# Batch 1's x loaded ahead of the weights, and its transposes and scores moved forward, in a cross-attention and maxout kernel

## The chip, the cores and the metric

The kernel runs on one core of a Trainium2 chip. Its time is the device time of one execution in microseconds; it stands as the median of several runs. The engines are named as the profile names them: PE (TensorE) for matmuls and transposes, with PEld for its weight loads, DVE (VectorE), ACT (ScalarE), POOL (GpSimd) and SP (SyncE, which here only issues DMAs).

## The reference

Attention in both directions between `x` (8 batches, 8 heads, 512 rows, 64 columns) and `state` (8, 8, 32, 64), and then a feed-forward layer with a maximum over three products:

```python
scores = scale * x @ state^T                    # per batch and head: 512 x 32
a      = softmax(scores, over the 32)
xread  = a @ state                              # 512 x 64
a2     = softmax(scale * state @ x^T, over the 512)
sread  = a2 @ x                                 # 32 x 64
attn   = concat([xread, sread], axis=rows)      # 544 rows, heads side by side: 512 columns
h      = max(attn @ w1, attn @ w2, attn @ w3)   # 512 -> 768
out    = h @ w_out                              # 768 -> 512
```

## The kernel before

Work goes by batch. For batch `b` the steps are these; the lines are those of the profile.

- `load_x(b)` (L70) loads x with a cast to bf16 through POOL's DMA queue. The x of batch 0 comes in two halves, one through SP as f32 (L79) that DVE casts (L392), one through POOL (L84).
- `x_transpose(b, g, copy)` (L159) transposes half of x on PE, eight 128x128 blocks into one PSUM tile; `copy`, on ACT or DVE, brings it to `xT` (L162). From batch 3 on `x_transpose_dma` does it by a DMA from SP's queue (L166).
- `scores(b, g0, g1)` (L180) multiplies xT with a block-diagonal form of the state (`bd`), and ACT takes the exponential into `e` (L185). `softmax` sums on DVE (`den`, L192), takes the reciprocal (`rden`, L194) and multiplies on POOL or DVE (`a`, L195).
- `a_transpose` (L206, copies L207) brings `a` to `aT`.
- `g_cols(b, ms)` (L281) multiplies the state with columns of the three weight matrices: G = state @ W. A column `m` stands for 128 of the 768, in all three matrices, and has one copy, of 128x768 (L287). Thereby xread @ W becomes aT @ G. `g_cols_fast` (L312, copies L317) is the same for the first column of batch 0, split between ACT and DVE. With `defer` a copy stands not at once but behind the first cast of the next maxout.
- `x_maxout(b, m)` (L327) makes the three products of one column, six matmuls into three PSUM tiles; ACT casts the first (L331), and two maxima on DVE follow (L334, L335), which give `ht`.
- `sread(b)` (L225) is the attention in the other direction; its result goes through a DMA transpose on SP's queue (L233). Its normaliser comes from a column of ones that stands behind x (L110).
- `ffn_out(b, j)` (L365) multiplies `ht` with `wout`, copies on ACT and stores.

The weights W1, W2, W3 come in four chunks of columns, three parts each (`load_w`, L104): chunks 0 and 1 have one column each, chunks 2 and 3 two. `keep_busy(n)` (L121) runs n matmuls of zeros.

Every engine works through its instructions in the order in which the program issues them. That order is written out by hand for batches 0 and 1; from batch 2 on a loop over `b` and six slots lays the next batch's preparation between the six maxouts of this one. PSUM tiles rotate in two rings: four tiles for tag `pw` (transposes, half scores, maxouts, sread, ffn) and two tiles for tag `two` (G columns, full scores, idle matmuls). A new tile waits until the last reader of the one four, or two, before it has ended.

The order by hand around the change, before:

```python
load_w(0); load_w(1); load_x(1)                     # POOL's queue, behind x of batch 0
...
softmax(0, 1, 2, nc.vector.tensor_mul); keep_busy(9)
a_transpose(0, 0, act); a_transpose(0, 1, dve)
g_cols_fast(0, 0); g_cols(0, (1,))
...
x_maxout(0, 0)
x_transpose(1, 0, act); x_transpose(1, 1, dve)
x_maxout(0, 1)
scores(1, 0, 1); scores(1, 1, 2)
```

Of the kernel before, what the change touches and what calls it, by code (L numbers as in the profile page):

```python
# [15 lines left out]
def kernel(  # L16
# [14 lines left out]
    nc = tc.nc  # L31
# [22 lines left out]
    dve, act, pool = nc.vector.tensor_copy, nc.scalar.copy, nc.gpsimd.tensor_copy  # L54
# [14 lines left out]
    def load_x(b):  # L69
        nc.gpsimd.dma_start(  # L70
            out=x_sb[b][:, 0:XW].rearrange("p (h jd) -> p h jd", h=H),
            in_=x[b].rearrange("h (p j) d -> p h (j d)", j=J))

    def x0_heads(g):
        return x[0].rearrange("(s g) (p j) d -> g p s (j d)", g=2, j=J)[g]
# [6 lines left out]
    ident = const.tile([128, 128], BF16, name="ident")  # L82
    make_identity(nc, ident)
    nc.gpsimd.dma_start(out=x0_sb[1], in_=x0_heads(1))  # L84

    chunks = ((0, 1), (1, 2), (2, 4), (4, 6))
    w_sb = wpool.tile([128, HS, NM * 384], BF16, name="w")
# [2 lines left out]
    def w_slices(t, c):  # L90
        m0, m1 = chunks[c]
        return t[:, :, 384 * m0:384 * m1].rearrange("p a (i mf) -> p a i mf", i=3)
# [7 lines left out]
    def load_w(c, parts=(0, 1, 2)):  # L100
        m0, m1 = chunks[c]
        for i in parts:
            w = (moe_w1, moe_w2, moe_w3)[i].rearrange("(kk p) f -> p kk f", p=128)
            nc.gpsimd.dma_start(out=w_slices(w_sb, c)[:, :, i, :], in_=w[:, :, m0 * 128:m1 * 128])  # L104

    load_w(0)
    load_w(1)
    load_x(1)
    for b in range(2):
        nc.gpsimd.memset(x_sb[b][:, XW:XW + D], 1.0)  # L110
    bds = [data.tile([128, 2, H, 2, Ns], BF16, name=f"bd{k}") for k in range(B // 2)]
    nc.vector.memset(bds[0], 0.0)

# [4 lines left out]
    def keep_busy(n):  # L118
        p = pp.tile([128, 1024], F32, tag="two", name="idle")
        for _ in range(n):  # L120
            nc.tensor.matmul(p[:, 0:512], zero[:, 0:128], zero, start=True, stop=True)  # L121


    def bd(b, h):
        return bds[b // 2][:, b % 2, h]
# [23 lines left out]
    def new(d, b, shape, name, bufs=2):  # L149
        d[b] = work.tile(shape, BF16, tag=name, bufs=bufs, name=name)  # L150

    def x_transpose(b, g, copy):

        if g == 0:
            new(xT, b, [128, H, 2, 128], "xT", bufs=3)
        p = pp.tile([128, HS, 2, 128], BF16, tag="pw", bufs=4, name="pxt")
        for s in range(HS):
            for jj in range(2):
                nc.tensor.transpose(  # L159
                    p[:, s, jj, :],  # L160
                    xv[b][:, 2 * s + g, 2 * jj:2 * jj + 2, :].rearrange("p j d -> p (j d)"), ident)
        copy(out=xT[b].rearrange("p (s g) j t -> p g s j t", g=2)[:, g], in_=p)  # L162
# [5 lines left out]
    def scores(b, g0, g1):  # L168
        n = g1 - g0
        if g0 == 0:  # L170
            new(e, b, [128, J, 2, HS, Ns], "e")
        if n == 2:
            p = pp.tile([128, J, n, HS, Ns], F32, tag="two", name="ps")
        else:
            p = pp.tile([128, J, n, HS, Ns], F32, tag="pw", bufs=4, name="psh")
        for jj in range(2):
            for g in range(g0, g1):
                for s in range(HS):
                    h = 2 * s + g
                    nc.tensor.matmul(  # L180
                        p[:, 2 * jj:2 * jj + 2, g - g0, s, :], xT[b][:, h, jj, :],
                        bd(b, h).rearrange("p c n -> p (c n)"),
                        start=(g == g0 and s == 0 and (n == 2 or jj == 0)),
                        stop=(g == g1 - 1 and s == HS - 1), skip_group_check=True)
        nc.scalar.activation(out=e[b][:, :, g0:g1], in_=p, func=AF.Exp, scale=scale)  # L185

    def softmax(b, g0, g1, mul):
        n = g1 - g0
        if g0 == 0:
            new(a, b, [128, J, 2, HS, Ns], "a")  # L190
        den = work.tile([128, J, n, HS], F32, tag=f"den{n}", name="den")
        nc.vector.reduce_sum(out=den, in_=e[b][:, :, g0:g1], axis=AX.X)  # L192
        rden = work.tile([128, J, n, HS], F32, tag=f"rden{n}", name="rden")
        nc.vector.reciprocal(out=rden, in_=den)  # L194
        mul(  # L195
            out=a[b][:, :, g0:g1].rearrange("p j g s n -> p j (g s) n"),
            in0=e[b][:, :, g0:g1].rearrange("p j g s n -> p j (g s) n"),
            in1=rden.rearrange("p j g s -> p j (g s)").unsqueeze(3).to_broadcast((128, J, n * HS, Ns)))

    def a_transpose(b, g, copy):  # L200

        if g == 0:
            new(aT, b, [128, J, 2, 128], "aT", bufs=3)
        p = pp.tile([128, J, 128], BF16, tag="pw", bufs=4, name="pat")
        for j in range(J):
            nc.tensor.transpose(p[:, j, :], a[b][:, j, g].rearrange("p s n -> p (s n)"), ident)  # L206
        copy(out=aT[b][:, :, g, :], in_=p)  # L207
# [31 lines left out]
    def flush_copies():  # L239
        while copies_due:  # L240
            copies_due.pop(0)()
# [30 lines left out]
    def g_cols(b, ms, copies=(act, act), defer=(False, False)):  # L272
        flush_copies()
        for m, copy, wait in zip(ms, copies, defer):
            if m == 0:
                new(G, b, [128, 2, NM * 384], "G", bufs=3)
            p = pp.tile([128, 2, 512], F32, tag="two", name="pg")
            pv = p[:, :, 0:384].rearrange("p g (i f) -> p g i f", i=3)
            for s in range(HS):
                for g in range(2):  # L280
                    nc.tensor.matmul(  # L281
                        pv[32 * s:32 * s + 32, g], bd(b, 2 * s + g)[64 * g:64 * g + 64, g, :],
                        m_cols(w_sb, m)[64 * g:64 * g + 64, s],
                        start=True, stop=True, tile_position=(64 * g, 32 * s))

            def place(m=m, pv=pv, copy=copy):
                copy(out=m_cols(G[b], m), in_=pv)  # L287

            if wait:
                copies_due.append(place)  # L290
            else:
                place()
# [12 lines left out]
    def g_cols_fast(b, m):  # L305

        if m == 0:
            new(G, b, [128, 2, NM * 384], "G", bufs=3)
        p = [pp.tile([128, 512], F32, tag="pw", bufs=4, name=f"pgf{g}") for g in range(2)]
        for s in range(HS):  # L310
            for g in range(2):
                nc.tensor.matmul(  # L312
                    p[g][32 * s:32 * s + 32, 0:384].rearrange("p (i f) -> p i f", i=3),
                    bd(b, 2 * s + g)[64 * g:64 * g + 64, g, :], m_cols(w_sb, m)[64 * g:64 * g + 64, s],
                    start=True, stop=True, tile_position=(64 * g, 32 * s))
        for g, copy in ((0, act), (1, dve)):
            copy(out=m_cols(G[b], m)[:, g], in_=p[g][:, 0:384].rearrange("p (i f) -> p i f", i=3))  # L317
# [19 lines left out]
    def x_maxout(b, m):  # L337
        maxout(b, m, 512,
               lambda i, k: m_cols(G[b], m)[:, k, i],
               lambda k: aT[b][:, :, k, :], 2)  # L340
# [52 lines left out]
    x_transpose(0, 0, dve)  # L393
    x_transpose(0, 1, dve)
    scores(0, 0, 1)
    load_w(2, (0, 1))
    softmax(0, 0, 1, nc.gpsimd.tensor_mul)
    scores(0, 1, 2)
    softmax(0, 1, 2, nc.vector.tensor_mul)
    keep_busy(9)  # L400
    a_transpose(0, 0, act)
    a_transpose(0, 1, dve)
    g_cols_fast(0, 0)
    g_cols(0, (1,))
    load_w(2, (2,))
    load_w(3)
    load_st(1, nc.gpsimd)
    load_x(2)
    x_maxout(0, 0)
    x_transpose(1, 0, act)  # L410
    x_transpose(1, 1, dve)
    x_maxout(0, 1)
    scores(1, 0, 1)
    scores(1, 1, 2)
    softmax(1, 0, 1, nc.gpsimd.tensor_mul)
    softmax(1, 1, 2, nc.gpsimd.tensor_mul)
    nc.gpsimd.dma_start(out=wout_sb, in_=moe_w_out.rearrange("(kk p) f -> p kk f", p=128))
    for k in range(2, B // 2):
        load_st(k, nc.gpsimd)
# [1 line left out]
    load_x(4)  # L421
    for b in range(2, B):
        nc.gpsimd.memset(x_sb[b][:, XW:XW + D], 1.0)
    sread(0)
    g_cols(0, (2, 3))
    g_cols(1, (0,))
    x_maxout(0, 2)
    a_transpose(1, 0, act)
    a_transpose(1, 1, act)
    g_cols(1, (1,))  # L430
    x_maxout(0, 3)
    x_maxout(1, 0)
    g_cols(0, (4, 5), defer=(False, True))
    x_maxout(1, 1)
    states_cast(1, pool)
    x_maxout(0, 4)
    sread(1)
    g_cols(1, (2, 3), defer=(False, True))
    x_maxout(0, 5)
    states(1, act)  # L440
    x_transpose(2, 0, dve)
    x_transpose(2, 1, act)
    x_maxout(1, 2)
    g_cols(1, (4, 5), defer=(False, True))
    x_maxout(1, 3)
    scores(2, 0, 2)
# [83 lines left out]
```

## Time and profile before

| | us |
|---|---|
| median of 5 runs | 159.21 |
| lowest to highest of them | 157.75 to 159.85 |
| the profiled execution, its own time | 158.32 |
| its span, first to last instruction | 156.5 |
| PE busy in the span | 147.1 |
| DVE, ACT, POOL busy | 98.1, 94.1, 50.5 |

How to read the views. A stage table gives, for a stretch of the span, each engine's busy time and its number of instructions, the granted clock of TensorE, the DMA share and the rate. A row of the timeline has start and duration in us, engine, line, operation, what is written and read, shapes and a count of merged instructions; in brackets the engine's idle time before it and what ended that. The duration of merged matmuls includes the modelled tail of the last one, so matmuls start sooner after each other than the durations say. In the chain of waits a row has start, length and the work on the path; a DMA stands there from issue to landing.

### The profile page before, as it was taken

What the parts mean: (1) busy time and instruction counts of PE and PEld (TensorE: products, weight loads), DVE (VectorE), ACT (ScalarE), POOL (GpSimd) and SP (SyncE); (2) the same over time, 40 slices, a digit from 0 to 9 for tenths busy, and PEclk for the clock granted to TensorE, in tenths of its full rate; (3) what the DMA queues carried; (4) which work ended last, traced back from release to release, by engine and by line L of the source; (5) the groups of instructions that cost most, each with busy time, mean ns of one, the idle gap of its engine ahead of it and who ended that gap; (6) DMA issues with size and microseconds to landing.
All of it is one profiled execution on the core that took longest, in us unless ns stands there. A gap on an engine that the chain in (4) does not pass through costs nothing.

```text
span 156.5 us, 3484 instructions
## 1 busy us (share of the span) xinstructions
PE 147.1 (94%) x1389; PEld 72.4 (46%) x1389; DVE 98.1 (63%) x172; ACT 94.1 (60%) x146; POOL 50.5 (32%) x72
## 2 busy tenths in 40 slices
PE   6788789999999999999999999999999999999990
PEld 2434443454454444444444444444444565665450
DVE  4685856868635866677567757775777583565110
ACT  3245697798747747773867386747774738333240
POOL 8998097000743405441014061501060100100150
PEclk9999999999999999999999999999999999999999
DMA  3999999999089999797930595070307030020374
GB/s 119 179 177 197 197 214 203 232 189 117 16 183 130 183 231 203 239 165 199 149 134 0 115 202 198 2 205 8 134 4 201 8 134 6 32 102 0 138 231 171
DMA packets 36720, 21.72 MB, mean 139 GB/s; under 512 B 21952, under 2 KB 34368, under 8 KB 36704
## 3 DMA queue, kind: packets, MB, share of 16 engines
q0 software_dynamic: 17216, 15.08, 49.4%
q1 hardware_dynamic: 19344, 6.29, 24.1%
q8 instruction: 11, 0.18, 0.5%
q10 hardware_dynamic: 144, 0.13, 0.2%
q14 instruction: 5, 0.04, 0.1%
HBM read 15.20 MB, written 8.91 MB: 154 GB/s over the span
## 4 chain that ended last, share of the span: by engine, by line
PE 77%; DMA 9%; ACT 6%; DVE 4%; issue 1%; POOL 1%; POOLq 0%; DVEq 0%; ACTq 0%
PE pw L327 40%; PE po L365 27%; DMA w<-in_moe_w_dram 5%; PE pg L255 4%; DMA x<-in_x_dram 4%; PE psr L225 2%; ACT t L331 2%; ACT G L287 2%; DVE t L334 2%; PE ps L180 1%; DVE den L192 1%; PE pg L281 1%; ACT e L185 1%; PE ph L357 1%; POOL a L195 1%
## 5 line engine op out<-in xcount | busy, mean ns | idle before, releaser
L327 PE MATMUL pw<-aT,G 128*128 128x512 bf16 x288 | 69.1, 380 | 0.6 <-ACT G L317 0.2
L334 DVE TENSOR_TENSOR t<-t,pw 128x512 bf16<-128x512 bf16 (+1 forms) x54 | 35.1, 650 | 33.2 <-ACT t L331 33.0
L365 PE MATMUL po<-wout,ht 128*128 128x512 bf16 x198 | 47.4, 380 | 0.2
L327 PEld LDWEIGHTS <-G 128*128 128x128 bf16 x288 | 27.0, 98 | 33.0 <-issue 3.6
L335 DVE TENSOR_TENSOR ht<-t,pw 128x512 bf16<-128x512 bf16 (+1 forms) x54 | 35.6, 658 | 5.6
L368 ACT COPY osb<-po 128x512 f32<-128x512 f32 x33 | 19.3, 585 | 29.8 <-PE po L365 29.8
L331 ACT CAST t<-pw 128x512 bf16<-128x512 f32 (+1 forms) x54 | 30.6, 567 | 8.3 <-PE pw L327 7.6
L365 PEld LDWEIGHTS <-ht 128*128 128x128 bf16 x198 | 18.8, 98 | 23.9 <-issue 2.8
L195 POOL TENSOR_TENSOR a<-e,rden 128x1024 bf16<-128x1024 bf16 (+1 forms) x9 | 14.5, 1618 | 40.0 <-DVE rden L194 29.7
L262 ACT CAST G<-pg 128x1024 bf16<-128x1024 f32 x24 | 24.5, 1022 | 3.8 <-PE pg L255 3.2
L377 POOL DMA_DIRECT2D out_dram<-osb x14 | 8.0, 569 | 46.1 <-ACT osb L368 35.7
L287 ACT CAST G<-pg 128x768 bf16<-128x768 f32 x11 | 8.7, 809 | 2.9 <-PE pg L281 2.9
L192 DVE TENSOR_REDUCE den<-e 128x32 f32<-128x1024 bf16 (+1 forms) x10 | 10.0, 996 | 0.5 <-ACT e L185 0.5
L104 POOL DMA_DIRECT2D w<-in_moe_w_dram x12 | 9.1, 785 | 0.0
L327 PE MATMUL pw<-ats,w 128*128 128x256 bf16 x72 | 8.8, 273 | 0.0
L185 ACT ACTIVATE e<-ps 128x1024 bf16<-128x1024 f32 x6 | 6.1, 1023 | 3.8 <-PE ps L180 3.7
L327 PEld LDWEIGHTS <-w 128*128 128x128 bf16 x72 | 7.0, 98 | 2.1
L255 PE MATMUL pg<-w,bd 64*32 64x512 bf16 x192 | 7.5, 381 | 0.0
L143 POOL COPY bd<-stT 64x512 bf16<-64x512 bf16 x4 | 4.3, 1070 | 9.3 <-DMA stT<-st 9.2
L121 PE MATMUL idle<-zero 128*128 128x512 bf16 x19 | 6.0, 467 | 1.2 <-DVE zero L81 1.2
L70 POOL DMA_DIRECT2D x<-in_x_dram x7 | 6.4, 915 | 0.6 <-DMA x<-in_x_dram 0.6
L180 PEld LDWEIGHTS <-xT 128*128 128x128 bf16 x128 | 4.8, 98 | 2.3 <-DVE xT L162 0.7
(54 smaller groups left out, 79.5 us busy)
## 6 DMA issues: line engine op xcount, KB each, us to landing
out_dram<-osb POOLq DMA_DIRECT2D x14, 512.0 KB, 3.1
x<-in_x_dram POOLq DMA_DIRECT2D x7, 512.0 KB, 10.2
w<-in_moe_w_dram POOLq DMA_DIRECT2D x6, 256.0 KB, 8.8
w<-in_moe_w_dram POOLq DMA_DIRECT2D x6, 128.0 KB, 5.9
wout<-in_moe_w_out_dram POOLq DMA_DIRECT2D x1, 768.0 KB, 8.6
x0f<-in_x_dram SPq DMA_DIRECT2D x1, 512.0 KB, 3.9
out_dram<-osb SPq DMA_DIRECT2D x1, 512.0 KB, 2.7
stf<-in_state_dram POOLq DMA_DIRECT2D x3, 128.0 KB, 8.5
```

The lines of the kernel that those rows point to most:

```text
L104: nc.gpsimd.dma_start(out=w_slices(w_sb, c)[:, :, i, :], in_=w[:, :, m0 * 128:m1 * 128])
L192: nc.vector.reduce_sum(out=den, in_=e[b][:, :, g0:g1], axis=AX.X)
L195: mul(out=a[b][:, :, g0:g1].rearrange("p j g s n -> p j (g s) n"), in0=e[b][:, :, g0:g1].rearrange("p j g s n -> p j (g s) n"), in1=rden.r ...
L255: nc.tensor.matmul(ps[g][32 * s:32 * s + 32], bd(b, 2 * s + g)[64 * g:64 * g + 64, g, :], w_sb[64 * g:64 * g + 64, s, c0:c1], start=True, ...
L262: copy(out=G[b][:, :, c0:c1], in_=p[:, :, 0:n])
L287: copy(out=m_cols(G[b], m), in_=pv)
L327: nc.tensor.matmul(p[:, 0:n], lhs(i, k), rhs(k), start=(k == 0), stop=(k == nk - 1))
L331: nc.scalar.copy(out=t0[:, 0:n], in_=pw[0][:, 0:n])
L334: nc.vector.tensor_max(t1[:, 0:n], t0[:, 0:n], pw[1][:, 0:n])
L335: nc.vector.tensor_max(ht[b][:, m, :], t1[:, 0:n], pw[2][:, 0:n])
L365: nc.tensor.matmul(p, ht[b][:, m, j * 128:(j + 1) * 128], wout_sb[:, m, :], start=(m == 0), stop=(m == NM - 1))
L368: act(out=o[:, j, :], in_=p)
```

## The change

The load of x of batch 1 goes right behind the second half of x of batch 0, ahead of all of W. The loads of chunks 2 and 3 of W stand together behind the first half of the softmax of batch 0. The first transpose of batch 1 stands between the idle matmuls (now 7 and 2), the first half of its scores ahead of the first G column of batch 0, the second transpose behind that column, and the second half of the scores behind the first maxout. The loads of the second state, of x of batch 2 and of what follows go behind the softmax of batch 1. The G columns, sread, transposes of `a` and maxouts of batches 0 and 1 are put in another order, some copies change between ACT and DVE, and more copies of G are deferred. The amount of work is the same.

```diff
     nc.gpsimd.dma_start(out=x0_sb[1], in_=x0_heads(1))
+    load_x(1)
...
     load_w(0)
-    load_w(1)
-    load_x(1)
     for b in range(2):
         nc.gpsimd.memset(x_sb[b][:, XW:XW + D], 1.0)
+    load_w(1)
...
     scores(0, 0, 1)
-    load_w(2, (0, 1))
     softmax(0, 0, 1, nc.gpsimd.tensor_mul)
+    load_w(2)
+    load_w(3)
     scores(0, 1, 2)
     softmax(0, 1, 2, nc.vector.tensor_mul)
-    keep_busy(9)
-    a_transpose(0, 0, act)
+    keep_busy(7)
+    x_transpose(1, 0, act)
+    keep_busy(2)
+    a_transpose(0, 0, dve)
     a_transpose(0, 1, dve)
+    scores(1, 0, 1)
     g_cols_fast(0, 0)
-    g_cols(0, (1,))
-    load_w(2, (2,))
-    load_w(3)
+    x_transpose(1, 1, dve)
+    softmax(1, 0, 1, nc.gpsimd.tensor_mul)
+    x_maxout(0, 0)
+    scores(1, 1, 2)
+    softmax(1, 1, 2, nc.gpsimd.tensor_mul)
     load_st(1, nc.gpsimd)
     load_x(2)
-    x_maxout(0, 0)
-    x_transpose(1, 0, act)
-    x_transpose(1, 1, dve)
-    x_maxout(0, 1)
-    scores(1, 0, 1)
-    scores(1, 1, 2)
-    softmax(1, 0, 1, nc.gpsimd.tensor_mul)
-    softmax(1, 1, 2, nc.gpsimd.tensor_mul)
     nc.gpsimd.dma_start(out=wout_sb, in_=moe_w_out.rearrange("(kk p) f -> p kk f", p=128))
...
         nc.gpsimd.memset(x_sb[b][:, XW:XW + D], 1.0)
+    g_cols(0, (1,))
+    g_cols(1, (0,))
     sread(0)
-    g_cols(0, (2, 3))
-    g_cols(1, (0,))
+    x_maxout(0, 1)
+    sread(1)
+    g_cols(1, (1,))
+    a_transpose(1, 0, act)
+    a_transpose(1, 1, dve)
+    g_cols(0, (2, 3), defer=(False, True))
+    x_maxout(1, 0)
+    x_maxout(1, 1)
     x_maxout(0, 2)
-    a_transpose(1, 0, act)
-    a_transpose(1, 1, act)
-    g_cols(1, (1,))
+    g_cols(1, (2, 3), defer=(False, True))
     x_maxout(0, 3)
-    x_maxout(1, 0)
     g_cols(0, (4, 5), defer=(False, True))
-    x_maxout(1, 1)
+    x_maxout(1, 2)
     states_cast(1, pool)
     x_maxout(0, 4)
-    sread(1)
-    g_cols(1, (2, 3), defer=(False, True))
-    x_maxout(0, 5)
     states(1, act)
     x_transpose(2, 0, dve)
     x_transpose(2, 1, act)
-    x_maxout(1, 2)
+    x_maxout(0, 5)
     g_cols(1, (4, 5), defer=(False, True))
     x_maxout(1, 3)
     scores(2, 0, 2)
```

## The prediction, made before the changed kernel was run

> **What bounds it now.** I read the stages first: busy time of each engine from the first slice of batch 0 (12.72 us) on, cut where the order written out by hand changes.
>
> ```profile
> core 0: us, PE busy (x) PEld busy (x) DVE busy (x) ACT busy (x) POOL busy (x), PEclk, DMA share, GB/s
> 12.72:22.70 9.98, 8.02 (x123) 4.79 (x124) 6.16 (x13) 7.11 (x12) 5.85 (x8) 1.00 1.44 203
> 22.70:35.78 13.08, 12.78 (x142) 5.91 (x142) 9.64 (x16) 10.65 (x18) 3.63 (x11) 1.00 1.43 205
> 35.78:43.80 8.02, 7.72 (x106) 4.13 (x105) 6.18 (x12) 6.26 (x9) 3.56 (x4) 1.00 0.54 78
> 43.80:151.53 107.73, 107.73 (x932) 52.26 (x932) 67.35 (x118) 64.14 (x99) 25.21 (x29) 1.00 0.57 125
> ```
>
> From 43.80 to 151.53 PE never stands, at clock 1.00. The change leaves that stage's work alone, so the time is the moment at which PE gets there plus a constant, and only standing of PE before it counts. Second, the timeline of the start, to see where it stands.
>
> ```profile
> 8.79 2.11 PE L121 MATMUL idle<-zero 128*128 128x512 bf16 x9
> ...
> 12.72 1.47 PE L327 MATMUL pw<-aT,G 128*128 128x512 bf16 x6 [0.23 <-ACT G L317]
> ...
> 14.70 1.07 PE L159 MATMUL pxt<-ident,x 128*128 128x128 bf16 x16 [0.50 <-DMA x<-in_x_dram]
> ...
> 15.35 1.01 ACT L162 COPY xT<-pxt 128x1024 bf16<-128x1024 bf16 x1 [1.40 <-PE pxt L159]
> ...
> 19.23 2.20 ACT L287 CAST G<-pg 128x768 bf16<-128x768 f32 x3 [0.81 <-PE pg L281]
> ...
> 20.08 0.36 PE L281 MATMUL pg<-w,bd 64*32 64x384 bf16 x8 [0.75 <-ACT G L287]
> ```
>
> See what stands in brackets: PE waits for x of batch 1 at 14.70, for W chunk 2 at 18.80, for ScalarE's copy of G at 20.08. Third, the chain of waits names the same W chunk, and the view of x's loads says when x of batch 1 lands: 6.91 + 7.7 = 14.65.
>
> ```profile
> 10.79 7.88 DMA w<-in_moe_w_dram
> 18.67 0.14 issue
> 18.80 0.40 PE pg L281 x8
> ```
>
> ```profile
> L70 POOL DMA_DIRECT2D x<-in_x_dram x1: 914/914/914, 6.9 to 6.9; - x1
> ...
> DMA to landing us min/median/max: 7.7/7.7/7.7
> ```
>
> PE's own work from 8.79 to scores(2) at 35.78, by start-to-start steps of the timeline: 9 idle matmuls at 0.216 (1.94); ten maxouts at 1.30 (13.0); twelve G columns at 0.225 (2.7); two sets of 16 transposes of x (0.9 each) and two of 8 of a (0.45 each); scores 0.48; two sread at 0.56; states 0.22. Sum 22.1 of 26.99: PE stands 4.9 us there. The edit removes and adds no work; it can only move that 4.9.
>
> **Loads.** GpSimd's loads land in order of issue, one after the other (issue from the timeline, time to landing from the view of each load's line): x of batch 0 at 7.10, six W parts of chunks 0 and 1 at 8.29 to 12.00 (0.74 apart, the first 1.19), x of batch 1 at 14.65 (2.65 after), chunk 2 at 15.96, 17.30, 18.67, chunk 3 at 20.61 to 23.01. With x of batch 1 second in the queue it lands at 7.10 + 2.65 = 9.75, or 10.2 if the first follower's extra 0.45 falls on it; chunk 0 at 12.0 to 12.4 (before 9.8); chunk 1 at 14.65 (before 12.0); chunk 2 as before, since the same bytes stand ahead. GpSimd issues x at 2.37, chunk 0 to 5.6, the ones, chunk 1 to 8.2; the multiplication of the first softmax starts at 9.79 as now, as it waits for rden; then six issues at 0.76 reach to 15.4. The queue still has chunk 1 in flight to 14.65, so chunk 2's first issue moved from 7.96 to 10.8 opens no hole. One issue can also be held by a landing: x of batch 2, the sixteenth load, waited 0.55 for the eighth, x of batch 1. Eight back, each load of the new order finds its predecessor landed (tightest: chunk 3's second at 13.9 behind 12.4, x of batch 3 at 21.9 behind 20.6). Behind these six stands the multiplication of softmax(1, 0): rden at 14.85, start 15.4; its taker asks at 18.9, so nothing. State 1, x of batch 2 and wout are issued at 18.3 to 20.7 (now 13.8 to 21.4), ahead of the queue's 23.0, so they land as now (23.3, 26.1, 30.0); the order asks for them at 24.4, 30 and 35. On SP's queue the transpose of batch 1's sread starts 20.0 instead of 30.7 and that of batch 0 at 17.7 instead of 20.5; batch 0's lay beside chunk 3's landings without moving them (1.08 and 1.32 apart), so 0; at worst 0.2, covered by 0.65 of slack at chunk 2's use.
>
> A rule weighs against the new load order: the Trainium skill, "DMA: Bandwidth & Descriptors", section "Anatomy of one DMA", prices a GpSimd load at 2.0 us plus bytes over 436 GB/s. By it x of batch 1 (1.05 MB read) would land 4.4 us after its issue, at 11.3 in the old order, and chunk 2 (0.52 MB a part, last issue 10.79) at 14.0, both before PE asks; no load need move, and the change would keep only its cost, the first slice 0.86 later (below): some +0.9. The row has 7.7 us, 14.65, and PE waiting for it; the measurement decides and I take the row.
>
> **The new order, step by step.** I carry PE, ScalarE and VectorE forward in program order, each operation with its row's duration: copy of eight transposes 1.01 (ACT) or 0.69 (DVE), exp of half 0.60, reduce 0.69 and reciprocal 0.25, copy of G 0.81, first cast of a maxout 0.59 on ACT (0.60 after the maxout starts), then two maxima of 0.69 on DVE; PSUM's pw ring of four and two ring of two free as those operations end.
> Idle matmuls to 10.30; x_transpose(1, 0) 10.30, its data there at 9.75 to 10.2; two idle ones 10.75; a_transposes 11.18 and 11.44 (VectorE's multiplication sets the second, as now); ScalarE has xT at 11.97; scores(1, 0) 12.02; first slice 12.25 (before 11.77), chunk 0 at 12.0 to 12.4. ScalarE runs exp(1, 0) to 13.05 before its half of the slice's copy, 13.53. So x_maxout(0, 0) starts 13.58, **0.86 later than now**. x_transpose(1, 1) hides in that wait. scores(1, 1) 14.88; G(0, 1) 15.12; G(1, 0) 15.35; sread(0) 15.6; ScalarE's exp to 15.9 and copy to 16.73, so x_maxout(0, 1) 16.78 (stand 0.6); sread(1) 18.08; G(1, 1), a_transposes, G(0, 2) 18.64 to 19.55; G(0, 3) 19.88, waiting for a PSUM tile (0.33); x_maxout(1, 0) 20.44, waiting for aT (0.34).
> Now compare like work. At 21.74 the new order has three maxouts done and also sread(1); the old one has three at 22.70 without it: 22.70 - (21.74 - 0.56) = **1.5 us ahead**. The gaps for x and W have gone, and ScalarE's copies are late in their place.
> On: (1, 1) 21.74, (0, 2) 23.27 (0.24 for VectorE, three maxouts in a row at 1.38 against PE's 1.30), G(1, 2..3) 24.56, (0, 3) 25.02, G(0, 4) 26.31, G(0, 5) 27.20 (0.67: its PSUM tile is freed by the deferred copy behind the cast), (1, 2) 27.43, (0, 4) 28.72, states and x_transpose(2) 30.06, (0, 5) 31.52 (0.3), G(1, 4..5) 32.81, (1, 3) 33.27, scores(2) 34.56 against 35.78: 1.2 ahead. ScalarE, behind by one cast, ends exp(2) at 36.5 against 37.54: 1.04 ahead. Between 35.8 and 43.8 PE shows small gaps behind that exp's softmax, so what arrives at 43.80 lies between; I take **1.1**. The DMA transposes that the loop needs (x of batch 3 lands 39.9, asked at 46.7) have 6 us of cover.
>
> **Sum.** The profiled execution took 158.32: 157.2. The five runs' median is 0.9 above it, by an unknown that I let stay: 159.21 - 1.1 = 158.1.
>
> **Rivals.** First, a larger gain. My four stands after 19.5 (0.33, 0.34, 0.24, 0.67, with 0.3 more: 1.9 in all) come from queues that I carried by hand; if casts slip in earlier, or the executions of the median wait longer for loads than the profiled one, three quarters come off: 2.5 gain, 156.7. For it: all W parts now have 0.4 to 3 us of slack where the old order met W and x on arrival. Against: ScalarE is 14.4 us busy in the 16.1 from 20.4 (eight G copies 6.5, eight casts 4.7, states 1.2, xT 1.0, exp 1.0), close to PE's 12.8 plus.
> Second, ScalarE becomes the bound of that stretch: another two stands like the 0.67 one, at each G pair; the gain is given back: 158.1 + 2 x 0.67 = 159.4.
> Third, slower: x of batch 1 lands together with the W behind it. PE takes matmuls in order, so x_transpose(1, 0) holds the a_transposes, the scores and the first slice of batch 0. Each microsecond after 10.30 costs one; at 11.4 the gain is gone, at 13.0 the loss passes 1%. If it shared the queue evenly with chunks 0 and 1 all would land at 14.65: 4.35 later, less the stands that this hides (about 1), 161.4. Against: the rows show separate landings in the order of issue.
> That the change misses its aim, x not landing early, is this same case.
>
> **How the numbers follow.** Forecast (gain 0.5 to 1.6) 0.45; larger gain 0.25; ScalarE bound 0.14; x late 0.16. A measurement of this kernel tells about 1%, 1.6 us, from no change. Faster: the larger gain and the forecast's edge, 0.30; slower: late x with a part of its cases short of 1%, and unseen stalls, 0.17; same 0.53. The likeliest case alone spans 157.3 to 158.9; the range, 156.2 to 160.7, adds the larger gain and the milder part of a late x, and leaves the rest of late x out.
>
> **What would show it.** Right: x of batch 1 landing before 10.3; first maxout near 13.6; no DMA as releaser of PE after 12.5; ACT G and DVE t in its place; scores(2) near 34.6; PE gap-free from about 42.7. Wrong: PE waiting for DMA x at 10.3, first slice after 13, or more standing of PE for ACT between 24 and 35 than 1.3 us.

## The result

The changed kernel takes 157.77 us (median of 41 executions, 156.57 to 160.51) against 158.47 us of the kernel before (76 executions): a ratio of 0.9955, 95% interval 0.9937 to 0.9973, so 0.7 us. Two more sets of executions, made beside the experiments below, gave 0.9919 (0.9894 to 0.9944) and 0.9949 (0.9920 to 0.9977). A ratio leaves out the executions that were over 1.5% above the fastest of their kernel, while a median here is that of all of them. The gain is real, under 1%, and lies between 0.7 and 1.3 us.

The head of the page after the change; the span before was 156.5 us, with 147.1 us of PE:

```profile
span 155.6 us, 3482 instructions
...
PE 147.9 (95%) x1389; PEld 72.8 (47%) x1389; DVE 98.8 (63%) x174; ACT 93.3 (60%) x144; POOL 50.9 (33%) x72
```

The stage table after the change, cut at the first maxout of batch 0, at scores(2), and at the ffn_out from which PE runs without a gap:

```profile
core 0: us, PE busy (x) PEld busy (x) DVE busy (x) ACT busy (x) POOL busy (x), PEclk, DMA share, GB/s
13.99:34.86 20.87, 19.83 (x248) 9.52 (x249) 15.97 (x31) 16.13 (x26) 9.98 (x19) 1.00 1.42 198
34.86:42.87 8.01, 7.71 (x105) 4.12 (x104) 6.16 (x11) 6.25 (x9) 3.56 (x4) 1.00 0.82 125
42.87:150.60 107.73, 107.73 (x932) 52.30 (x932) 67.32 (x118) 64.13 (x99) 25.21 (x29) 1.00 0.55 125
```

The last stage has 107.73 us before and after, to the hundredth, and the stage ahead of it 8.02 and 8.01: nothing behind scores(2) takes another time. PE reaches it at 42.87 instead of 43.80, 0.93 earlier, and the span is 0.9 shorter. All of the gain is made before scores(2), at 34.86 instead of 35.78. The timeline of PE shows what it waits for there now:

```profile
10.80 0.62 PE L159 MATMUL pxt<-ident,x 128*128 128x128 bf16 x8 [0.44 <-DMA x<-in_x_dram]
...
13.99 1.47 PE L327 MATMUL pw<-aT,G 128*128 128x512 bf16 x6
...
17.08 1.47 PE L327 MATMUL pw<-aT,G 128*128 128x512 bf16 x6 [0.37 <-ACT G L287]
...
27.25 0.35 PE L281 MATMUL pg<-w,bd 64*32 64x384 bf16 x8 [0.26 <-ACT G L287]
```

The waits for x at 14.7 and for W at 18.8 are gone; the second of them is this row of PE's timeline before:

```profile
18.80 0.52 PE L281 MATMUL pg<-w,bd 64*32 64x384 bf16 x16 [0.55 <-DMA w<-in_moe_w_dram]
```

There is one short wait for x at 10.8, and then ScalarE's copies of G. In the chain of waits the early path now begins with the load of x of batch 1, from its issue at 2.38 to its landing at 10.76, and passes through its transpose and ScalarE's copy of it:

```profile
2.38 8.38 DMA x<-in_x_dram
10.76 0.05 issue
10.80 0.64 PE pxt L159 x8
11.46 1.02 ACT xT L162
```

### The profile page after: what moved, and what is told of

Its sections match the earlier page's. It is cut to its first block, busy times and chain, and to the rows that moved or that the text cites. A ratio compares the mean times of both kernels' runs of the same rounds, so it can differ in the third digit from the quotient of the medians.

```text
span 155.6 us, 3482 instructions
## 1 busy us (share of the span) xinstructions
PE 147.9 (95%) x1389; PEld 72.8 (47%) x1389; DVE 98.8 (63%) x174; ACT 93.3 (60%) x144; POOL 50.9 (33%) x72
## 4 chain that ended last, share of the span: by engine, by line
PE 82%; ACT 6%; DMA 5%; DVE 2%; issue 1%; POOL 1%; POOLq 0%; ACTq 0%
PE pw L327 43%; PE po L365 27%; DMA x<-in_x_dram 5%; PE pg L255 4%; PE psr L225 2%; ACT G L287 2%; PE ps L180 1%; ACT t L331 1%; PE pxt L159 1%; ACT e L185 1%; PE pg L281 1%; PE ph L357 1%; DVE den L192 1%; ACT xT L162 1%; ACT aT L207 1%
## 5 line engine op out<-in xcount | busy, mean ns | idle before, releaser
L365 PEld LDWEIGHTS <-ht 128*128 128x128 bf16 x198 | 18.8, 98 | 23.9 <-issue 2.8
L121 PE MATMUL idle<-zero 128*128 128x512 bf16 x19 | 6.9, 512 | 1.2 <-DVE zero L81 1.2
## 6 DMA issues: line engine op xcount, KB each, us to landing
stf<-in_state_dram POOLq DMA_DIRECT2D x3, 128.0 KB, 10.3
```

The costliest lines, as they stand in the source:

```text
L365: nc.tensor.matmul(p, ht[b][:, m, j * 128:(j + 1) * 128], wout_sb[:, m, :], start=(m == 0), stop=(m == NM - 1))
```

## The experiments

Three theories were to be told apart: that the load of x, the early transposes and scores, and the new order of the rest need each other (mine); that the load alone is the gain; that the order alone is. In the tables of times, "first maxout" is the first matmul of x_maxout(0, 0).

**The loads alone.** The kernel before, with `load_x(1)` ahead of W and nothing else moved:

```diff
     nc.gpsimd.dma_start(out=x0_sb[1], in_=x0_heads(1))
+    load_x(1)
...
     load_w(0)
-    load_w(1)
-    load_x(1)
     for b in range(2):
         nc.gpsimd.memset(x_sb[b][:, XW:XW + D], 1.0)
+    load_w(1)
```

> The kernel before with the loads' order alone changed: x of batch 1 ahead of all of W; the order of the other engines' work is that of before. My theory (the early x pays only because the transposes and scores are put where it arrives, and W pays for it): x lands at 10.8, chunk 0 at 12.9, chunk 1 at 15.1 as after the change; PE then stands for chunk 1 at G(0, 1), which here is ahead of the first maxout, so that this starts at about 15.6 instead of 12.7, and the kernel is some 1.2 us slower than before (159.7). Rival (the early load is the gain, since PE no longer waits for x at 14.7): 0.5 us faster than before (158.0).

Measured: 162.36 us (four executions), ratio 1.0168 (1.0078 to 1.0258). Slower than before, as my theory had it, but by over twice what I expected. From PE's timeline of this kernel, then a row of POOL's and a stage row of the same execution:

```profile
12.94 0.62 PE L206 MATMUL pat<-ident,a 128*128 128x128 bf16 x8 [1.94 <-POOL a L195]
...
15.28 0.52 PE L281 MATMUL pg<-w,bd 64*32 64x384 bf16 x8 [1.41 <-DMA w<-in_moe_w_dram]
```

```profile
11.06 0.75 POOL L105 DMA_DIRECT2D w<-in_moe_w_dram  x1 [2.10 <-DVE rden L194]
```

```profile
13.70:20.50 6.80, 5.39 (x40) 2.96 (x33) 2.47 (x5) 3.10 (x5) 3.59 (x5) 0.50 1.47 196
```

The wait for chunk 1 of W at 15.28 is the expected one, and the first maxout starts at 15.74. The wait at 12.94 was not expected: two loads of chunk 2 stand ahead of the softmax's multiplication on POOL, and the second of them was issued only at 11.06, 0.3 after x of batch 1 had landed. (The bracket names `rden`; that the load waited for x is shown by the POOL experiment below.) Behind these stands the clock fell to one half from 13.7 to 20.5, so that the maxout's six matmuls took 2.5 us. The mean clock was 0.978 in three of the four executions; in the fourth it was 1.000, and this one took 160.01 us, 1.6 above before and so nearer to the 1.2 expected. It has no profile; but it suggests that most of what I had left out is the clock. The early load by itself is a loss either way.

**The order alone.** The changed kernel, with x of batch 1 loaded behind chunks 0 and 1 as before:

```diff
     nc.gpsimd.dma_start(out=x0_sb[1], in_=x0_heads(1))
-    load_x(1)
...
     load_w(0)
+    load_w(1)
+    load_x(1)
     for b in range(2):
         nc.gpsimd.memset(x_sb[b][:, XW:XW + D], 1.0)
-    load_w(1)
```

> The changed kernel with the loads of before: x of batch 1 behind chunks 0 and 1 of W. My theory: x lands at 14.65, PE stands there at x_transpose(1, 0) with batch 0's a_transposes and first slice behind it, the first maxout comes 3.6 us later than after the change (17.6), and the kernel is 3.4 us slower than after it (161.2). Rival (the order of G columns and maxouts between 17 and 35 us is the gain, x has cover): within 0.5 us of after (158).

Measured: 162.42 us, ratio 1.0225 (1.0158 to 1.0292). From PE's timeline:

```profile
14.70 1.03 PE L159 MATMUL pxt<-ident,x 128*128 128x128 bf16 x8 [4.82 <-DMA x<-in_x_dram]
```

One row tells it: PE stands 4.82 us for x, and eight transposes that take 0.62 at full clock take 1.03. The order without the load loses, and by more than expected; the expected number had no clock in it.

**x between the two chunks.** The same edit with `load_x(1)` between `load_w(0)` and `load_w(1)`.

> The changed kernel with x of batch 1 between chunks 0 and 1 of W. My theory (each microsecond of x costs one): x lands at 12.4 to 12.9, 1.6 to 2.1 later than after the change, and the kernel is 1.5 to 1.9 us slower than after it (159.5). Rival (a stall of that length is taken up by the later stands of PE for ScalarE): 0.5 us slower at most.

Measured: 160.70 us, ratio 1.0135 (1.0076 to 1.0194); against the 0.9955 of the change that is 1.8%, or 2.9 us. The row of PE's timeline, and then the stretch behind it in a stage table of the same kernel:

```profile
12.29 0.62 PE L159 MATMUL pxt<-ident,x 128*128 128x128 bf16 x8 [2.27 <-DMA x<-in_x_dram]
```

```profile
12.80:16.20 3.40, 3.40 (x36) 2.43 (x34) 1.41 (x3) 1.98 (x3) 2.43 (x4) 0.50 1.49 186
```

x landed at 12.24, 1.5 later than after the change; scores(2) came at 37.09, 2.2 later. The surplus of 0.7 is the clock of 0.50 through 3.4 us, in which PE's rows are up to 1.7 times as long. Put beside the executions of the changed kernel itself, in which x lands at different times, the five profiles give the slope:

| kernel | x of batch 1 lands | first maxout | scores(2) | span |
|---|---|---|---|---|
| changed, second set | 10.06 | 13.36 | 34.22 | 154.9 |
| changed, third set | 10.42 | 13.69 | 34.55 | 155.2 |
| changed | 10.76 | 13.99 | 34.86 | 155.6 |
| x between the chunks | 12.24 | 16.23 | 37.09 | 158.4 |
| x behind both chunks | 14.65 | 18.92 | 39.78 | 160.4 |

From 10.06 to 10.76 each 0.1 us of x is 0.09 at scores(2) and 0.1 in the span. Beyond, a microsecond costs 1.5 at scores(2) in the fourth row and 1.3 in the fifth, since the clock falls. The span ends 120.7 to 120.8 us behind scores(2) in four of the five rows; in the fourth row it is 121.3, and the 0.5 more come behind the start of PE's last matmul, in the closing copy and store.

**The changed kernel again**, for the two later sets:

> The changed kernel unaltered, as the measure for the others of this set. Both theories: 0.7 us faster than before (157.8).

Measured: 156.98 us, ratio 0.9919 (0.9894 to 0.9944).

> The changed kernel unaltered, as the measure for the others of this set: 0.7 to 1.3 us faster than before, as its two earlier sets showed.

Measured: 157.73 us, ratio 0.9949 (0.9920 to 0.9977).

**The front alone.** The changed kernel up to the scores of batch 1, then the order of before:

```diff
     g_cols(0, (1,))
-    g_cols(1, (0,))
-    sread(0)
     x_maxout(0, 1)
-    sread(1)
-    g_cols(1, (1,))
-    a_transpose(1, 0, act)
-    a_transpose(1, 1, dve)
-    g_cols(0, (2, 3), defer=(False, True))
-    x_maxout(1, 0)
...
+    sread(0)
+    g_cols(0, (2, 3))
+    g_cols(1, (0,))
+    x_maxout(0, 2)
+    a_transpose(1, 0, act)
+    a_transpose(1, 1, act)
+    g_cols(1, (1,))
+    x_maxout(0, 3)
...
```

> The changed kernel up to the scores of batch 1, and from the second maxout on the order of before for the G columns, sread, a_transposes and maxouts of batches 0 and 1. Theory (both halves of the reordering are needed: the new order of the second half keeps PE busy until chunk 2 of W has landed): G(0, 2) is asked for at about 18.7, chunk 2's third part lands at 19.4, PE stands 0.7 there and again for the G copies, scores(2) comes 0.6 to 1.2 later than in the changed kernel: no faster than before by over 0.3 us (158.2). Rival (the early transposes and scores alone bring the gain): within 0.2 us of the changed kernel.

Measured: 159.38 us, ratio to before 1.0043 (1.0012 to 1.0074), while the changed kernel of the same set had 0.9949. PE's timeline:

```profile
17.05 1.47 PE L327 MATMUL pw<-aT,G 128*128 128x512 bf16 x6 [1.09 <-ACT G L287]
...
19.43 0.52 PE L281 MATMUL pg<-w,bd 64*32 64x384 bf16 x16 [0.36 <-DMA w<-in_moe_w_dram]
...
20.70 0.36 PE L281 MATMUL pg<-w,bd 64*32 64x384 bf16 x8 [0.75 <-ACT G L287]
```

In this profile x landed at 10.72 and the first maxout started at 13.96, as in the changed kernel's; yet scores(2) came at 36.41 instead of 34.86. So 1.5 us hang on the second half of the order. The rows name the stands: nothing stands between G(0, 1) and its maxout to cover ScalarE's copy, W of chunk 2 is asked for as it lands, and three G columns in a row wait for a PSUM tile. Expected was 0.6 to 1.2; the first of these stands I had not counted. The copies that change between ACT and DVE and the added deferrals were not tried alone.

**POOL's order.** Chunk 2's first two parts ahead of the first multiplication, as before the change:

```diff
+    load_w(2, (0, 1))
     softmax(0, 0, 1, nc.gpsimd.tensor_mul)
-    load_w(2)
+    load_w(2, (2,))
     load_w(3)
```

> The changed kernel with two parts of chunk 2 issued again ahead of the first softmax's multiplication on GpSimd, as before the change. Theory (a load waits for the landing of the one eight loads earlier, and what stands behind it on GpSimd waits too; the profile of the kernel with the loads' order alone showed GpSimd held from 9.0 to 11.1): the second part is the tenth load and waits for x of batch 1, 10.8, the multiplication starts at 11.8 instead of 10.05, the a_transposes at 12.9 instead of 11.7, the first maxout 0.9 later. Rival (GpSimd's wait is hidden behind PE's for x): a_transposes at 11.7 as now.

One execution, 159.15 us. A row of POOL's timeline, then one of PE's:

```profile
12.04 0.74 POOL L105 DMA_DIRECT2D w<-in_moe_w_dram  x1 [2.94 <-DMA x<-in_x_dram]
```

```profile
13.91 0.62 PE L206 MATMUL pat<-ident,a 128*128 128x128 bf16 x8 [1.06 <-POOL a L195]
```

The tenth load waits for the landing of x, the second load, which in this execution came at 11.75; the multiplication behind it on POOL starts at 12.79, and PE stands another 1.06 for it. (That x itself landed 1.0 later than in the change's profile cannot be put down to this edit from a single execution.) So the move of chunk 2's loads behind the softmax belongs to the move of x. This is also the unexpected wait of the first experiment.

**x in two halves.** Only the even heads are needed at 10.3, so they go ahead of chunk 0 and the odd ones behind it:

```diff
-    load_x(1)
+    load_half(1, 0)          # heads 0, 2, 4, 6
...
     load_w(0)
+    load_half(1, 1)          # heads 1, 3, 5, 7
```

> The changed kernel with x of batch 1 loaded in two halves: the heads that x_transpose(1, 0) takes ahead of chunk 0 of W, the others behind chunk 0. My theory: the first half lands at about 8.7, chunk 0 at 11.3, the second half at 12.7; PE's stands of 0.44 for x and 0.26 for chunk 0 go, x_maxout(0, 0) starts at 13.5 instead of 14.0, scores(2) at 34.5, and the kernel is 0.3 us faster than after the change. Rival (ScalarE's queue takes up such a gain, as it did between 20 and 35 us): no difference from after, 0.1 at most.

Measured: 157.18 us, ratio 0.9931 (0.9902 to 0.9960). The start did better than expected: the first half landed at 7.65 instead of 8.7, chunk 0 at 9.9 instead of 11.3, no wait for a load is left, the first maxout started at 13.04 and scores(2) at 33.90, 0.96 ahead of the changed kernel's profile. But the span was 156.1, not 154.6. The timelines of POOL and of PE say where it went:

```profile
60.42 2.17 POOL L150 COPY bd<-stT 64x512 bf16<-64x512 bf16 x2 [7.31 <-DMA stT<-st]
```

```profile
62.64 0.63 PE L187 MATMUL ps<-bd,xT 128*128 128x64 bf16 x16 [1.17 <-POOL bd L150]
```

scores(4) needs the block-diagonal state of batches 4 and 5. Its DMA transpose landed at 60.4, POOL's two copies ended at 62.6, and PE, whose maxout before it was through at 61.3, stood for 1.3. In the three profiles of the changed kernel the copies began at 58.2 to 58.5 and there was no stand. The transpose of x of batch 4, which stands ahead of it on SP's queue, took 12.3 us to land here and 9.6 to 10.5 there; why is not shown. Again, beside the changed kernel's third set:

> The kernel with x of batch 1 in two halves around chunk 0, again, now beside the changed kernel on one chip. Theory (the first maxout no longer waits for x and chunk 0): 0.3 to 0.5 us faster than the changed kernel. Rival (what the start gains, the stand for bd at scores(4) takes, in part of the executions): no difference.

Measured: 156.91 us, ratio to before 0.9897 (0.9832 to 0.9962); the changed kernel there had 0.9949 (0.9920 to 0.9977). The intervals overlap, so I do not call the halves faster than the change; the two sets lean that way. This profile had the stand at scores(4) too. But three of its six executions, of which no profile was kept, had a span of 154.5 to 154.6 us, which is what the gain at the start leaves if nothing stands; so the stand may be missing in some.

**Taking that stand away.** The transpose of state pair 2 goes ahead on SP's queue, right behind its cast, in the changed kernel:

```diff
     for k in range(2, B // 2):
         states_cast(k, pool)
+    state_transpose_dma(2)      # was issued in the loop, behind aT of batch 3
```

> The changed kernel with one move in the loop's stage: the DMA transpose of state pair 2 goes on SP's queue ahead of the transpose of x of batch 4 and of aT of batch 3 (it stood behind them, at 55.4). Theory (part of the gain is lost where scores(4) waits for bd of states 2, as the profile of the half-load kernel shows with 1.55 us at 61 us, while the changed kernel's profile shows 1.8 us of slack): bd is there by 57 instead of 60.4 to 62.6, no execution stands there, and the median is 0.3 to 0.8 us below that of the changed kernel (157.2), with the lowest times unmoved. Rival (the scatter of 4 us between executions comes from the start, the loads): no difference.

Measured: 164.44 us, ratio 1.0412 (1.0360 to 1.0463). The theory's means failed: bd was there at 55.6, but everything behind it on SP's queue came late. From PE's timeline:

```profile
65.49 2.72 PE L334 MATMUL pw<-aT,G 128*128 128x512 bf16 x6 [5.08 <-DMA aT<-a]
```

The transpose of x of batch 4 took 14.9 us to land where it had taken 9.6 to 10.5 in the changed kernel, that of aT of batch 3 took 11.9 instead of 3.5 to 4.5 and landed at 65.4 instead of 57.6, and PE stood for 5.1 us. Why the transposes became so slow is not shown.

> Both: x of batch 1 in two halves around chunk 0, and the earlier transpose of state pair 2. Theory: scores(2) at 34 as with the halves alone, no stand at scores(4), so 0.9 us of the start arrive at the end: 156.4 to 156.8. Rival (ScalarE or the loop takes it up): as the halves alone, 157.2.

Measured, with both edits: 164.19 us, ratio 1.0358 (1.0309 to 1.0407), with the same stand (4.87 us for aT).

**The slice ahead of the exponential.** In the kernel with two halves, `g_cols_fast(0, 0)` changes places with `scores(1, 0, 1)`.

> The two halves, and the first G column of batch 0 ahead of the first half of batch 1's scores, so that ScalarE copies it before that exponential. Theory (ScalarE's exp(1, 0) of 0.6 us delays the first maxout): x_maxout(0, 0) at 12.6 instead of 13.04, and of this 0.2 to 0.4 us at the end: 0.3 us faster than the two halves alone. Rival (x_maxout(0, 1) waits for ScalarE's copy behind both exponentials anyway): no difference.

Measured: 156.80 us, ratio to before 0.9899 (0.9832 to 0.9966). The first maxout started at 12.61 and scores(2) at 33.46, as the theory had it, 0.3 and more earlier than with the halves alone. The time does not show it: in the profile PE stood at 59.9 for aT and at 62.5 for bd. What the start gains from here on, the loop's transposes take back in the profiled executions.

The best kernels of the study are the last one and the halves alone, at 156.8 and 156.9 us against 158.84 of before in their set; between them, and from the changed kernel, they are not separated.

## Why the prediction was right, and where it was off

**The frame held.** It was that only PE's standing before the loop counts. The stage of 107.73 us is the same before and after, and the gain at scores(2), 0.92, arrives at the end as 0.9. Forecast was 1.1; the profiles show 0.93, the ratios of the three sets 0.7 to 1.3. The absolute forecast of 158.1 came nearer to the 157.77 than its parts deserve: the median of five that it started from was 0.74 above that of 76, and the gain was put 0.4 above that of the first set, so that half of the first error was taken back by the second. That is luck.

**Its own signs.** Two of the things that were named as signs of being wrong came: PE waited for x at 10.3, until 10.80, and the first slice started at 13.03. The forecast held all the same, since only 0.30 us of the delay was left at scores(2).

**x of batch 1: the term that was mis-sized.** I took 2.65 us from the landing of x of batch 0 to that of x of batch 1, and got 9.75 to 10.2. In the profile it was 4.35 (6.41 to 10.76), in the second and third sets 3.7 and 4.0. That it did not cost 1.7 us is luck again: x of batch 0 landed at 6.41 instead of the 7.10 of before, for a reason that no run shows.

The 2.65 was no transfer time but the distance of two landings. Loads that land one after the other need not move one after the other. The view of DMA queues tells what moved between the two landings, before (12.00 to 14.65) and after (6.41 to 10.76):

```profile
DMA packets 1038, 0.52 MB, mean 197 GB/s; under 512 B 19, under 2 KB 1038, under 8 KB 1038
```

```profile
DMA packets 1918, 0.71 MB, mean 163 GB/s; under 512 B 1027, under 2 KB 1918, under 8 KB 1918
```

x moves in packets of 512 bytes (4 rows of 64 columns in bf16), chunks 0 and 1 of W in packets of 256 (128 columns). So over half of the packets were W's, 0.26 MB, which moved beside the last ones of x. At 197 GB/s the 0.71 MB would have taken 3.6 us: of the error of 1.7 us, about 1.0 is the W that moved along and 0.7 the lower rate (an estimate from these two rows). The rate is lowest at the start of the stretch. From 6 to 8 us, in stage tables of before, of the changed kernel and of its second set:

```profile
6.00:8.00 2.00, 1.42 (x24) 1.12 (x24) 0.89 (x2) 0.00 (x0) 2.00 (x6) 1.00 1.41 135
```

```profile
6.00:8.00 2.00, 1.66 (x22) 1.39 (x22) 0.96 (x3) 0.00 (x0) 2.00 (x5) 1.00 1.02 131
```

```profile
6.00:8.00 2.00, 1.57 (x25) 1.18 (x24) 1.28 (x3) 0.04 (x1) 2.00 (x5) 1.00 1.30 171
```

The last column is the rate. The 135 stood in the profile of before, where I could have read it. At 171 x landed at 10.06, at 131 at 10.76; but this rate does not settle the landing, for in the POOL experiment it was 156 and x landed at 11.75.

The error carried on: x_transpose(1, 0) at 10.80 instead of 10.30, chunk 0 at 12.9 instead of 12.0 to 12.4, the first slice at 13.03 instead of 12.25, the first maxout at 13.99 instead of 13.58.

**The steps behind it** nearly kept their distance; of the 0.41 at the first maxout, 0.30 was left at scores(2):

| start of | forecast | measured |
|---|---|---|
| x_maxout(0, 1) | 16.78 | 17.08 |
| x_maxout(1, 0) | 20.44 | 20.80 |
| x_maxout(0, 3) | 25.02 | 25.23 |
| G(0, 5), behind the deferred copy | 27.20 | 27.25 |
| x_maxout(0, 5) | 31.52 | 31.72 |
| scores(2) | 34.56 | 34.86 |

The stands for ScalarE came where they were placed, and were shorter: 0.37 at 17.08 where I had 0.6, then for aT ahead of 20.80, and 0.26 for the deferred G copy at 27.25 where I had 0.67. The one of 0.33 at G(0, 3) came as about 0.2, inside a merged row of PE's timeline whose bracket does not show it; the other pairs of G columns have 0.52:

```profile
19.88 0.79 PE L281 MATMUL pg<-w,bd 64*32 64x384 bf16 x16
```

Of the 0.24 among three maxouts in a row, under 0.1 came. I also had ScalarE's first cast 0.60 behind the start of its maxout, where the rows of before have 0.65 (12.72 and 13.37, 15.60 and 16.26); beside the rest this is small.

**The other loads** came 0.5 to 0.9 later than placed: chunk 1 complete at 15.13, chunk 2 at 19.56, chunk 3 at 23.78. The slack I counted covered that here; in the second set PE waited 0.25 for chunk 2 at 19.56. That chunk 2's later issue opens no hole held: its first part landed 1.32 behind chunk 1. The wait for the eighth load back held as drawn, and the POOL experiment shows it as a cost of some 1 us that the change avoids by moving chunk 2 with x.

**The rule and the row.** I kept the row's issue-to-landing of 7.7 us against the estimate of 4.4 us from the fit in the Trainium skill, "DMA: Bandwidth & Descriptors", section "Anatomy of one DMA". After the change x took 8.4, second in the queue. By that estimate the reordering would have had no gain; the two experiments with a later x show that it hangs on when x lands.

**The rivals.** x landing together with the W behind it came true in part, as the packets show, though the landings kept the order of issue. The late x was right in its slope but too mild in price: x at 14.65 was put at 161.4 and gave 162.4; that PE's clock falls behind such a stand was left out. ScalarE as a new bound did not come. The larger gain is seen at the start of the kernels with two halves, not safely at the end. The 0.9 us by which the median of five runs lay over the profiled execution shrank to 0.15 with 76 runs; so it was scatter.

## What to carry to other kernels

When a load is moved ahead, price it in the stretch of the queue where it will lie, not where it lay; the distance between two landings is not a transfer time, since the next loads can move beside the last packets of this one. Count what every other user of that queue, the loads and the engine's own work behind them, loses. A load and the order of its users are one change: here each half alone cost 1.7% and 2.3%, and the front without the new order behind it still lost 0.4%, while together they gained 0.5 to 0.8%. Before trimming a start further, look for the next chain with little slack; here it was a state transpose at 60 us, with 0.7 to 1.8 us of it in the profiles of before and of the change.

## What the runs showed of the hardware that I had not expected

- The same load at the same place in the queue has no fixed landing: x of batch 1, second in POOL's queue and whole, landed at 10.06 to 11.75 us in seven profiles, of the changed kernel and of four others. From the landing of x of batch 0 on the queue moved 163 to 179 GB/s in all seven; what differs is how much it moved before x was complete: 0.64 to 0.65 MB in 3.7 to 3.8 us, 0.69 to 0.73 in 3.8 to 4.4, and 0.93 in 5.4. x's own share can be no more than 0.52; the rest is W. Why x's last packets come so late, and why the rate between 6 and 8 us varies from 131 to 182 GB/s in these profiles, stays open.
- TensorE's clock can fall behind a stand of 2 us, and does not always. Behind a stand of 2.27 us it was 0.50 for the next 3.4 us, as the stage row of that kernel shows; behind stands of 1.94 and 1.41 us it was 0.50 for 6.8 us in the profile of the loads alone, while one of that kernel's four executions kept 1.000; behind stands of 1.78 and 1.06 us, in the POOL experiment, it stayed at 1.00. So a late load cost up to 1.5 times its delay here.
- The same DMA transpose can take much longer to land when another is put ahead of it. With one of 128x512 put ahead of it, the transpose of x of batch 4 took 14.9 us to land in the changed kernel, against 9.6 to 10.5 without, and 13.3 in the kernel with halves, against 12.2 to 12.5; the one of aT behind it took 11.9 against 3.5 to 4.5, and 11.7 against 6.6 to 7.0. They ran beside stores and loads of x; which of these does it was not tried.
